# Loading the first two x tiles as two column halves, and moving half of their transposes behind the first products

## The chip, the cores and the metric

One core of a Trainium2 chip runs the whole kernel. The metric is the device time of one execution in microseconds (us); lower is better. The kernel before has a median of 104.45 us over three runs (104.1, 104.45 and 105.25).

A core has five engines that run side by side and meet through semaphores: TensorE (PE, with its weight loads listed apart as PEld), VectorE (DVE), ScalarE (ACT), GpSimd (POOL) and SyncE (SP). Transfers between the large memory and the core's own memory are issued here from two rings, SyncE's (SP) and ScalarE's (ACT), and all of them run on the same 16 DMA engines.

## The reference

A dense layer, the Mish activation, and a second dense layer. x is 2048 x 512, w1 is 512 x 1792, w2 is 1792 x 512, all bf16:

```python
h = einsum("bsd,df->bsf", x, w1) + b1
sp = log1p(exp(-abs(h))) + where(h > 0, h, 0)
act = h * tanh(sp)
return einsum("bsf,fd->bsd", act, w2)
```

## The kernel before

The 2048 tokens are worked in four blocks of 512. For each block the first dense layer makes 14 tiles `f` of 128 hidden columns; each is the sum of four products over `k`, the four 128-wide pieces of the 512 input columns (`mm1_step`, L189). ScalarE turns a finished tile into its activation (`mish`, L172). Then the second dense layer makes four token tiles, each a sum of 14 products of 512 columns (`mm2_step`, L212). Token tile 3 is the exception: its share of `f` = 1 is computed on VectorE (L230, L233) during the whole run and added at the end.

TensorE needs x with the input columns on the partitions, so x has to be transposed. For tokens 256 and up a transposing DMA does that. Tokens 0 to 255 (token tiles j = 0 and j = 1, the first to be needed) come in their natural layout by one plain load into `x_nat` (256 KB, L119) and are transposed by TensorE: `transpose_x` (L145) multiplies 64-row halves by a 64 x 64 identity, 16 instructions in all (L156), and VectorE and ScalarE copy the results from PSUM into `xT` (L164). The first products wait for these copies and for the first piece of w1.

The start of the kernel is written out by hand. Seven fills (L113) multiply constants into a PSUM bank that nobody reads; they keep TensorE busy until x arrives. w1's columns for `f` 0 to 7 (`OPEN` = 8) come as four loads of 256 KB, one per `k`: k 0 and k 2 on ScalarE's ring (L118), k 1 and k 3 on SyncE's (L120, L123). SyncE's ring carries, in this order: `x_nat`, k 1, the transposing load of tokens 256 to 511 (token tiles 2 and 3, `t_x23`, L122, which first waits for the third fill), k 3, b1, the rest of w1, and w2 in one load.

The products of block 0 are ordered by `first(fs, js, ks)`, which runs over k, then over f, for the token tiles in js: eight products of 128 columns (f 0 to 3, j 0, then j 1, k 0), then products of 256 columns for both j together (f 4 to 7 with k 0, then all eight f with k 1 and k 2), then 24 for token tiles 2 and 3 with k 0 to 2, and then eight of 512 columns with k 3, each of which completes a tile of `f`:

```python
first(range(4), (0,), (0,))
first(range(4), (1,), (0,))
first(range(4, OPEN), (0, 1), (0,))
first(range(OPEN), (0, 1), (1, 2))
first(range(OPEN), (2, 3), (0, 1, 2))
first(range(OPEN), None, (3,), True)
```

Tile `f` accumulates in PSUM bank `f % 8`; the transposes use banks 0 to 7 in pairs before that, and the first product into a bank waits for the copy that empties it.

## Time and profile before

| | us |
|---|---|
| median of three runs | 104.45 |
| the profiled execution | 104.08 |
| its span, first to last instruction | 102.7 |
| TensorE busy in it | 99.6 (97% of the span) |
| VectorE busy | 80.0 (78%) |
| ScalarE busy | 48.2 (47%) |
| DMA engines, moved in all | 24.76 MB at a mean of 241 GB/s |

The profile lists instructions with the line of the kernel that made them; a line can be that of a helper, so every load has line L93. Times are counted from the span's start. Matmuls are pipelined: the listed duration of one runs from its start to its modelled end and overlaps the next, so the rate of a stream of products is read from the distance of their starts. A few matmul records are missing from the trace. A share of the 16 DMA engines can come out above 100% in a short window, since a packet counts whole where it starts.

### The profile page before, as it was taken

The numbers are of one execution on the slowest core, as the hardware profiler recorded it, in microseconds if no ns is written. First come the engines' busy times: TensorE is split into PE (matmuls) and PEld (weight loads), VectorE is DVE, ScalarE is ACT, GpSimd is POOL, SyncE is SP. The second block draws the span as 40 slices with busy tenths as digits, with TensorE's granted clock in tenths as the row PEclk, the third lists the DMA queues.
The fourth block names the chain that finished last, engine by engine and source line by source line (L and its number), as shares of the span: only waits on it lengthen the run. The fifth ranks groups of instructions, "written<-read, shape, count | busy, mean of one in ns | idle before, by whom it ended". The sixth has DMA issues, their size and how long they took to land.

```text
span 102.7 us, 1352 instructions
## 1 busy us (share of the span) xinstructions
PE 99.6 (97%) x518; PEld 48.7 (47%) x527; DVE 80.0 (78%) x142; ACT 48.2 (47%) x75; POOL 0.4 (0%) x5
## 2 busy tenths in 40 slices
PE   6999999999999999999999999999999999999993
PEld 2587444444444444444444444444444444444472
DVE  1203000695979599999999999999999999999972
ACT  4301999220777781022588872222277776210210
POOL 1000000000000000000000000000000000000000
PEclk9999999999999999999999999999999999999999
DMA  2999999999799999789496838497857839111103
GB/s 62 371 281 359 366 262 360 255 330 228 303 273 228 378 429 373 201 325 297 184 320 172 338 73 364 105 347 224 293 153 306 284 124 341 67 57 51 51 0 102
DMA packets 15442, 24.76 MB, mean 241 GB/s; under 512 B 8396, under 2 KB 12748, under 8 KB 13388
## 3 DMA queue, kind: packets, MB, share of 16 engines
q1 hardware_dynamic: 15004, 24.12, 72.8%
q10 hardware_dynamic: 432, 0.56, 1.5%
q8 instruction: 4, 0.07, 0.2%
q14 instruction: 2, 0.02, 0.1%
HBM read 20.71 MB, written 2.10 MB: 222 GB/s over the span
## 4 chain that ended last, share of the span: by engine, by line
PE 97%; issue 1%; DVE 0%
PE ps L189 47%; PE ps L212 47%; PE ps L113 3%; PE ps L156 1%; DVE o_sb L271 0%
## 5 line engine op out<-in xcount | busy, mean ns | idle before, releaser
L233 DVE SCALAR_TENSOR_TENSOR acc<-w_bc,a_tok,acc 128x448 f32<-128x448 bf16 x126 | 75.4, 681 | 3.0 <-DMA w_bc<-in_w_dram 3.0
L189 PE MATMUL ps<-xT,w_sb 128*128 128x512 bf16 (+2 forms) x247 | 48.8, 355 | 0.4
L212 PE MATMUL ps<-w_sb,a_sb 128*128 128x512 bf16 (+3 forms) x248 | 48.7, 354 | 0.2
L172 ACT ACTIVATE a_sb<-ps,b_sb 128x512 bf16<-128x512 f32 x56 | 37.2, 698 | 12.8 <-PE ps L189 7.6
L189 PEld LDWEIGHTS ps<-xT,w_sb 128*128 128x128 bf16 x252 | 24.2, 98 | 24.2 <-DVE xT L164 0.3
L212 PEld LDWEIGHTS ps<-w_sb,a_sb 128*128 128x128 bf16 x252 | 23.1, 98 | 25.5 <-issue 0.3
L247 ACT ACTIVATE o_sb<-ps 128x512 bf16<-128x512 f32 x14 | 8.4, 598 | 32.7 <-PE ps L212 32.7
L230 DVE TENSOR_SCALAR acc<-w_bc,a_tok 128x448 f32<-128x448 bf16 x2 | 0.8, 450 | 10.4 <-DMA w_bc<-in_w_dram 10.4
L113 PE MATMUL ps<-const-bfloat16-1.0 128*128 128x512 bf16 (+1 forms) x7 | 2.7, 563 | 0.8 <-PEq L355 0.8
L289 DVE STREAM_TRANSPOSE b_T<-b_nat 32x32 bf16<-32x32 bf16 x4 | 0.8, 202 | 3.3 <-DMA b_nat<-in_b_dram 3.2
L164 DVE CAST xT<-ps 128x128 bf16<-128x128 f32 (+1 forms) x2 | 0.6, 352 | 2.4 <-PE ps L156 2.4
L271 ACT ACTIVATE o_sb<-ps 128x320 bf16<-128x320 f32 x1 | 0.4, 438 | 4.1 <-PE ps L212 4.1
L113 PEld LDWEIGHTS ps<-const-bfloat16-1.0 128*128 128x128 bf16 x7 | 0.9, 135 | 2.1 <-issue 2.1
L164 ACT ACTIVATE xT<-ps 128x256 bf16<-128x256 f32 (+1 forms) x3 | 0.9, 347 | 1.8 <-PE ps L156 1.7
L115 ACT ACT_TABLE_LOAD x1 | 1.3, 1283 | 0.7 <-PEq L355 0.7
L271 DVE CAST o_sb<-ps 128x128 bf16<-128x128 f32 (+1 forms) x2 | 0.5, 258 | 1.1 <-PE ps L212 1.0
L110 DVE MEMSET b_nat<- 32x64 uint32 x1 | 0.1, 112 | 0.8 <-PEq L355 0.8
L243 DVE TENSOR_TENSOR o_sb<-ps,acc 128x448 bf16<-128x448 f32 x1 | 0.6, 625 | 0.1
L241 DVE TENSOR_TENSOR acc<-acc 128x448 f32<-128x448 f32 x1 | 0.6, 624 | 0.0
L156 PEld LDWEIGHTS ps<-ident,x_nat 64*128 64x128 bf16 x16 | 0.5, 123 | 0.4 <-DMA x_nat<-in_x_dram 0.4
L156 PE MATMUL ps<-ident,x_nat 64*128 64x64 bf16 x16 | 0.6, 237 | 0.0
L139 DVE TENSOR_SCALAR ident<-diff 128x128 bf16<-128x128 int32 x1 | 0.2, 227 | 0.2 <-POOL diff L137 0.2
(7 smaller groups left out, 1.0 us busy)
## 6 DMA issues: line engine op xcount, KB each, us to landing
w_bc<-in_w_dram SPq DMA_DIRECT2D x16, 1024.0 KB, 4.9
out_dram<-o_sb SPq DMA_DIRECT2D x15, 128.0 KB, 2.3
w_sb<-in_w_dram SPq DMA_DIRECT2D x1, 1792.0 KB, 11.0
w_sb<-in_w_dram SPq DMA_DIRECT2D x1, 768.0 KB, 5.8
w_sb<-in_w_dram ACTq DMA_DIRECT2D x2, 256.0 KB, 3.7
w_sb<-in_w_dram SPq DMA_DIRECT2D x2, 256.0 KB, 3.6
x_nat<-in_x_dram SPq DMA_DIRECT2D x1, 256.0 KB, 2.6
out_dram<-o_sb SPq DMA_DIRECT2D x1, 80.0 KB, 1.6
```

The lines of the kernel that those rows point to most:

```text
L113: t_fill = [pe.mark(nc.tensor.matmul(ps[:, 7, 0:n], c_w, c_m[:, 0:n], start=True, stop=True)) for n in WARM]
L115: act.eng.preload_act_table(ACT.Mish)
L156: mm = nc.tensor.matmul(ps[:, b0 + h, lo:lo + H], x_nat[g, j, k * P:(k + 1) * P], ident[g, g], start=True, stop=True)
L164: t = eng.mark(nc.vector.tensor_copy(dst, src) if eng is dve else act.eng.activation(dst, src, ACT.Copy))
L172: t = act.mark(act.eng.activation(a_sb[:, f, starts[s]:starts[s + 1]], ps[:, bank, 0:n], ACT.Mish, bias=b1_sb[:, f:f + 1]))
L189: return nc.tensor.matmul(ps[:, bank, lo:hi], w1_sb[:, k, f * P:(f + 1) * P], xT[:, k, starts[s] + lo:starts[s] + hi], start=first, stop=( ...
L212: return nc.tensor.matmul(ps[:, bank, c:hi - lo], a_sb[:, f, i * P:(i + 1) * P], w2_sb[:, f, lo + c:hi], start=(f == 0), stop=(f == FT - 1))
L230: t = dve.mark(nc.vector.tensor_scalar(o, w, col, None, ALU.mult))
L233: t = dve.mark(nc.vector.scalar_tensor_tensor(o, w, col, o, ALU.mult, ALU.add))
L247: t = [act.mark(act.eng.activation(dst, src, ACT.Copy))]
L271: t = eng.mark(nc.vector.tensor_copy(dst, src) if eng is dve else act.eng.activation(dst, src, ACT.Copy))
L289: t = dve.mark(nc.vector.transpose(b1_T[j * SQ:(j + 1) * SQ, :], b1_nat[:, j * SQ:(j + 1) * SQ]))
```

## The change

The load of `x_nat` is cut into two loads, columns 0 to 255 (k 0 and 1) and columns 256 to 511 (k 2 and 3), each with its own semaphore. The load of w1's k 1 moves from SyncE's ring to ScalarE's. `transpose_x` does k 0 and 1 alone; one fill of 256 columns (`KEEP`) follows it, and one of the fills ahead of it is dropped and another made shorter. After the first eight products TensorE waits for the second half of `x_nat` and transposes its four 128 x 128 tiles (k 2 and 3, j 0 and 1) in whole tiles into bank 6; ScalarE copies them out in two instructions. Since bank 6 is taken by then, the products of `f` = 6 with k 0 and k 1 come after those of the other seven.

```diff
-WARM = (512,) * 5 + (256,) * 2
+WARM = (512,) * 5 + (128,)
+KEEP = (256,)
...
-        for k in (0, 2):
+        for k in (0, 1, 2):
             load_part(act, k, k + 1, 0, OPEN)
-        t_xn = load(sp, x_nat[:, :, :], x2[0:2 * P, :].rearrange("(p j) d -> p j d", p=P), "s_xn")
-        load_part(sp, 1, 2, 0, OPEN)
+        xv = x2[0:2 * P, :].rearrange("(p j) d -> p j d", p=P)
+        t_xn = [load(sp, x_nat[:, :, c:c + D // 2], xv[:, :, c:c + D // 2], "s_xn%d" % c) for c in (0, D // 2)]
         sp.wait(t_fill[2])
...
-            for b0, eng, js, ks in ((0, dve, (0,), (0,)), (2, act, (1,), (0,)), (4, dve, (0, 1), (1,)), (6, act, (0, 1), (2, 3))):
+            for b0, eng, js, ks in groups:
...
-        transpose_x()
+        transpose_x(t_xn[0], ((0, dve, (0,), (0,)), (2, act, (1,), (0,)), (4, dve, (0, 1), (1,))))
+        for n in KEEP:
+            fill(n)
         t_b1c = spread_b1()
         first(range(4), (0,), (0,))
         first(range(4), (1,), (0,))
-        first(range(4, OPEN), (0, 1), (0,))
-        first(range(OPEN), (0, 1), (1, 2))
+        pe.wait(t_xn[1])
+        for k in (2, 3):
+            for j in (0, 1):
+                lo = (k - 2) * 2 * P + j * P
+                mm = nc.tensor.matmul(ps[:, 6, lo:lo + P], x_nat[:, j, k * P:(k + 1) * P], ident[:, :], start=True, stop=True)
+        act.wait(pe.mark(mm))
+        for k in (2, 3):
+            t = act.mark(act.eng.activation(xT[:, k, 0:2 * P], ps[:, 6, (k - 2) * 2 * P:(k - 1) * 2 * P], ACT.Copy))
+            t_cp[0, k] = t_cp[1, k] = t
+        free[6] = [t]
+        first((4, 5, 7), (0, 1), (0,))
+        first((0, 1, 2, 3, 4, 5, 7), (0, 1), (1,))
+        first((6,), (0, 1), (0, 1))
+        first(range(OPEN), (0, 1), (2,))
```

TensorE's queue at the start of the program, before the change (a name is output <- input; `ps` is PSUM, and the last number of a shape is the columns):

```order
L113 MATMUL ps<-const-bfloat16-1.0 128x512 x5
L113 MATMUL ps<-const-bfloat16-1.0 128x256 x2
L156 MATMUL ps<-ident,x_nat 128x64 x16
L189 MATMUL ps<-xT,w_sb 128x128 x8
L189 MATMUL ps<-xT,w_sb 128x256 x44
L189 MATMUL ps<-xT,w_sb 128x512 x32
```

And with the change:

```order
L116 MATMUL ps<-const-bfloat16-1.0 128x512 x5
L116 MATMUL ps<-const-bfloat16-1.0 128x128
L161 MATMUL ps<-ident,x_nat 128x64 x8
L116 MATMUL ps<-const-bfloat16-1.0 128x256
L194 MATMUL ps<-xT,w_sb 128x128 x8
L308 MATMUL ps<-ident,x_nat 128x128 x4
L194 MATMUL ps<-xT,w_sb 128x256 x44
L194 MATMUL ps<-xT,w_sb 128x512 x32
```

Eight of the sixteen half transposes are gone from ahead of the products, four whole ones stand between the eighth and the ninth product, and the products themselves are the same in number and size; a fill of 256 columns stands just ahead of the first product.

SyncE's queue at the start, which issues only transfers, before the change:

```order
L93 DMA x_nat<-in_x_dram 128x1024
L93 DMA w_sb<-in_w_dram 128x1024
L93 DMA_TRANSPOSE xT<-in_x_dram 128x4x256
L93 DMA w_sb<-in_w_dram 128x1024
L93 DMA b_nat<-in_b_dram 14x128
L93 DMA w_sb<-in_w_dram 128x4x768
L93 DMA w_sb<-in_w_dram 128x14x512
```

And with the change:

```order
L94 DMA x_nat<-in_x_dram 128x2x256 x2
L94 DMA_TRANSPOSE xT<-in_x_dram 128x4x256
L94 DMA w_sb<-in_w_dram 128x1024
L94 DMA b_nat<-in_b_dram 14x128
L94 DMA w_sb<-in_w_dram 128x4x768
L94 DMA w_sb<-in_w_dram 128x14x512
```

The first load is now two, and its pieces are runs of 256 elements (512 bytes) where they were runs of 1024 elements (2048 bytes); the load of w1's k 1 that stood second is gone from this queue, and ScalarE issues three such loads, k 0, 1 and 2, where it issued two.

More of the change, by code (lines that the diff above doesn't have):

```diff
@@ L112, in bass_standalone__dense_activation_mish__prompt_kernel, with fill @@
         c_m = nc.const_aps.tensor(1.0, [P, 512], BF)
-        t_fill = [pe.mark(nc.tensor.matmul(ps[:, 7, 0:n], c_w, c_m[:, 0:n], start=True, stop=True)) for n in WARM]
+        def fill(n):
+            return nc.tensor.matmul(ps[:, 7, 0:n], c_w, c_m[:, 0:n], start=True, stop=True)
+        t_fill = [pe.mark(fill(n)) for n in WARM]
         act.eng.preload_act_table(ACT.Mish)
         act.wait(t_bz)
-        for k in (0, 2):
+        for k in (0, 1, 2):
             load_part(act, k, k + 1, 0, OPEN)
-        t_xn = load(sp, x_nat[:, :, :], x2[0:2 * P, :].rearrange("(p j) d -> p j d", p=P), "s_xn")
-        load_part(sp, 1, 2, 0, OPEN)
+        xv = x2[0:2 * P, :].rearrange("(p j) d -> p j d", p=P)
+        t_xn = [load(sp, x_nat[:, :, c:c + D // 2], xv[:, :, c:c + D // 2], "s_xn%d" % c) for c in (0, D // 2)]
         sp.wait(t_fill[2])
@@ L143, in bass_standalone__dense_activation_mish__prompt_kernel, with transpose_x @@
         t_mish = {}
-        def transpose_x():
-            pe.wait(t_xn, t_id)
+        def transpose_x(t, groups):
+            pe.wait(t, t_id)
             H = P // 2
-            for b0, eng, js, ks in ((0, dve, (0,), (0,)), (2, act, (1,), (0,)), (4, dve, (0, 1), (1,)), (6, act, (0, 1), (2, 3))):
+            for b0, eng, js, ks in groups:
                 m = len(js)
```

## The prediction

> **What bounds the kernel now.** I read the page first, then the chain of waits in order of time, then the start instruction by instruction. The page says how little there is to win:
>
> ```profile
> PE 99.6 (97%) x518; PEld 48.7 (47%) x527; DVE 80.0 (78%) x142; ACT 48.2 (47%) x75; POOL 0.4 (0%) x5
> ```
>
> The chain of waits (start, length, who) shows where TensorE (PE) is not yet on products:
>
> ```profile
> 0.77 2.71 PE ps L113 x7
> 3.49 0.54 PE ps L156 x16
> 4.03 0.13 issue
> 4.16 5.42 PE ps L189 x52
> 9.58 0.05 issue
> 9.64 6.85 PE ps L189 x31
> ```
>
> Fills, then the transposes, then from 4.16 us products without a break (the pieces of 0.05 are missing records). So the end moves one for one with two things: the start of the first product, and whatever TensorE does after it that is not a product. The change touches both.
>
> What releases the first product stands in three views: the timeline of the start, the DMA issues one by one (KB, us from issue to landing), and the groups by shape for the copies.
>
> ```profile
> 0.74 0.40 SPq L93 DMA_DIRECT2D x_nat<-in_x_dram  x1
> 0.95 0.86 ACTq L93 DMA_DIRECT2D w_sb<-in_w_dram  x2
> 1.20 0.41 SPq L93 DMA_DIRECT2D w_sb<-in_w_dram  x1
> 1.36 0.46 ACTq L93 DMA_DIRECT2D w_sb<-in_w_dram  x1
> 2.24 1.30 SPq L93 DMA_TRANSPOSE xT<-in_x_dram  x1
> 5.18 0.50 SPq L93 DMA_DIRECT2D w_sb<-in_w_dram  x1
> ...
> 3.70 0.62 DVE L164 CAST xT<-ps 128x128 bf16<-128x128 f32 x2 [2.38 <-PE ps L156]
> 3.75 0.98 ACT L164 ACTIVATE xT<-ps 128x128 bf16<-128x128 f32 x3 [1.73 <-PE ps L156]
> ...
> x_nat<-in_x_dram SPq DMA_DIRECT2D x1, 256.0 KB, 2.6
> w_sb<-in_w_dram ACTq DMA_DIRECT2D x1, 256.0 KB, 3.1
> w_sb<-in_w_dram SPq DMA_DIRECT2D x1, 256.0 KB, 3.5
> w_sb<-in_w_dram ACTq DMA_DIRECT2D x1, 256.0 KB, 4.3
> xT<-in_x_dram SPq DMA_TRANSPOSE x1, 4.3
> w_sb<-in_w_dram SPq DMA_DIRECT2D x1, 1792.0 KB, 11.0
> ...
> L164 DVE CAST xT<-ps 128x128 bf16<-128x128 f32 x1 | 0.3, 291 | 2.4 <-PE ps L156 2.4
> ```
>
> Issue plus landing time: x_nat at 3.34, k 0 (0.95) at 4.05, k 1 (1.20) at 4.70, k 2 (1.36) at 5.66, the transposed tiles 2 and 3 (2.24) at 6.54, w2 (5.18) at 16.18. VectorE's first copy ends at 3.70 + 0.29 = 3.99. So **two things** release the first product at 4.16, about 0.1 us earlier: the copy at 3.99 and k 0 at 4.05. Bringing x forward alone would do nothing; k 0 has to move too.
>
> **The transfers.** They run one after another at full rate. In windows of the DMA view (packets, MB, share of 16 engines) only one ring is at work:
>
> ```profile
> q1 hardware_dynamic: 67, 0.14, 103.7%
> q10 hardware_dynamic: 79, 0.16, 101.3%
> q1 hardware_dynamic: 672, 0.17, 127.8%
> ```
>
> The first is 3.68 to 4.02 us (SyncE's ring, w1 k 1), the second 4.36 to 4.80 (ScalarE's, k 2), the third 5.14 to 5.74 (SyncE's, the transposing load). A packet of 2048 bytes takes 1.037 x 16 x 0.34 / 67 = 84 ns of one engine, one of 256 bytes 1.278 x 16 x 0.60 / 672 = 18 ns. The change makes x's packets 512 bytes, which no row shows. On the straight line between these two it is 28 ns; the bounds are 18 and 84. I take 28, since 512 lies near the 256 end.
>
> - x_nat took 128 x 84 / 16 = 0.67 us of all engines. One half is 256 packets of 28 ns: 0.45 us. So the first half is through 0.22 us earlier, and k 0 behind it also.
> - Both halves take 0.90 us, so everything behind them is **0.22 us later**: k 2 at 5.88, tiles 2 and 3 at 6.76, w2 at 16.40. k 1 loses its place to the second half and follows it: 4.70 + 0.22 = 4.92. That second half lands 0.45 behind k 0: 3.83 + 0.45 = 4.28.
>
> First half at 3.12, VectorE's first copy at 3.77, k 0 at 3.83: the first product starts at 4.16 - 0.22 = **3.94**. The fills are out of the way: five of 512 columns and one of 128 end near 3.0 (next rows). The added fill of 256 columns runs while the copies do.
>
> **The clock.** The page's PEclk row reads full speed throughout, but the distances do not:
>
> ```profile
> 2.43 0.15 PEld L113 LDWEIGHTS ps<-const-bfloat16-1.0 128*128 128x128 bf16 x1 [0.28 <-issue]
> 2.86 0.15 PEld L113 LDWEIGHTS ps<-const-bfloat16-1.0 128*128 128x128 bf16 x1 [0.28 <-issue]
> 3.42 0.24 PE L156 MATMUL ps<-ident,x_nat 64*128 64x64 bf16 x2
> 3.79 0.24 PE L156 MATMUL ps<-ident,x_nat 64*128 64x64 bf16 x2
> 4.16 0.23 PE L189 MATMUL ps<-xT,w_sb 128*128 128x128 bf16 x1
> 4.39 0.50 PE L189 MATMUL ps<-xT,w_sb 128*128 128x128 bf16 x5
> 4.83 0.49 PE L189 MATMUL ps<-xT,w_sb 128*128 128x256 bf16 x3
> 5.71 0.49 PE L189 MATMUL ps<-xT,w_sb 128*128 128x256 bf16 x3
> 15.89 0.59 PE L189 MATMUL ps<-xT,w_sb 128*128 128x512 bf16 x2
> 16.33 0.38 PE L212 MATMUL ps<-w_sb,a_sb 128*128 128x512 bf16 x1
> ```
>
> Fills of 512 columns stand 0.43 us apart; products of 512 later 0.22 (15.89 to 16.33 holds two), of 256 0.11 (4.83 to 5.71 holds eight), of 128 from 4.16 on 0.057 (four by 4.39). The transposes still ran at half speed: eight pairs of 64 columns from 3.42 to 3.79, 0.053 a pair. So full speed came between 3.8 and 4.2, just as the products began: the products start free of the slow stretch by a hair. A start at 3.94 lies in it.
>
> I take the grant at 4.18. From 3.94 to 4.18 products of 128 take 0.11 us: 2.2 of the eight. The other 5.8 take 0.32, so the eight end at **4.50**, where before they ended at 4.16 + 8 x 0.057 = 4.62. Of the 0.22 us of head start 0.12 is left. Were the grant at 3.9, all of it would be.
>
> The Trainium skill (TensorE: Matmul & The Clock Gate, Part 1: The HAM clock gate) has the same rule: half clock until TensorE has been busy for a window of about 3.4 us; 0.77 + 3.4 = 4.2 agrees with the spacings. It also calls the window free-running, so that the moment varies from run to run; one trace cannot show that.
>
> **The transposes in the stream.** Ahead of the products, transposes cost nothing, since the first product waits for VectorE and k 0. Behind the eighth product they are TensorE time: four of 128 columns at the products' rate, 4 x 0.057 = **0.23 us**. The wait ahead of them is free: the half is there at 4.28, the eight end at 4.50. ScalarE's two copies end well ahead of the products with k 2: ScalarE starts 0.33 after TensorE's first transpose in the rows above (3.42 to 3.75) and needs 0.98 for three copies, so near 5.8; the first product that needs them or bank 6 comes later, as follows.
>
> **The sum on TensorE.** After: eight products by 4.50, transposes to 4.73, then the same 44 of 256 columns. Before these began at 4.62. Net **+0.11 us**. Then the later transfers have to be in time:
> - k 1 is wanted at 4.73 + 3 x 0.11 = 5.06 and lands at 4.92: 0.14 ahead, where a landing released a product after some 0.1.
> - bank 6 and k 2 are wanted after 12 products, at 6.05; k 2 lands at 5.88 and frees a product at 5.98.
> - tiles 2 and 3: wanted at 6.93, there at 6.76.
> - w2: the first L212 moves from 16.33 to 16.44; w2 lands at 16.40 and frees it at 16.50. Before, it had 0.15 to spare, now it is 0.06 late.
>
> No cover is more than 0.1 us thick, so I add 0.05 for the most likely miss: **+0.16 us**. VectorE's chain for tile 3 starts up to 0.22 later; at its end there is more room than that:
>
> ```profile
> L271 DVE CAST o_sb<-ps 128x128 bf16<-128x128 f32 x1 | 0.3, 292 | 1.0 <-PE ps L212 1.0
> ```
>
> VectorE sat idle for 1.0 us before the last copies.
>
> The sum against the profiled execution: 104.08 + 0.16 = 104.24. Its 104.08 is 0.37 under the median of the three runs; against the median the forecast is 104.45 + 0.16 = **104.6**.
>
> **The rivals.**
>
> *Slower: k 2 falls behind the transposing load.* Before, the rings alternated: x (SP), k 0 (ACT), k 1 (SP), k 2 (ACT), tiles 2 and 3 (SP). The windows above show whole transfers in turn, which fits two rules, order of issue or turn by turn between the rings; before, both give the same sequence. With the change SP holds both halves and then tiles 2 and 3, ACT holds k 0, 1, 2. By order of issue k 2 (issued near 1.8) stays ahead; turn by turn it is half, k 0, half, k 1, *tiles 2 and 3*, k 2. The transposing load moves 262144 / 256 = 1024 packets, 1024 / 672 x 0.60 = 0.91 us. Then k 2 lands at 5.88 + 0.91 = 6.79, its product starts at 6.89 instead of 6.05: a hole of 0.84, with the 0.11 a total of +0.95: **105.4**. If the load gives way after a part of its packets, the hole shrinks; under a fifth of them none is left. Against it: nothing in the trace of before. For it also nothing: it decides at k 1's end, and before that case never arose. The Trainium skill (DMA: Bandwidth & Descriptors, Queues, rings and completion order) says that an engine alternates between rings packet by packet, a packet being some 9 to 17 pieces and at most 64; no run so far shows it. By that rule a part of the load, up to all of it, goes first.
>
> *Slower still: full speed comes one stretch later.* From the first fill to the grant were 3.4 us. The fills ahead of x shrink from 3072 columns to 2688 plus 256 behind the transposes, and there is a pause for x near 3.0 and one for k 0. If that leaves TensorE too idle for the grant at 4.2, another 3.4 us run at half speed: 1.7 us of products lost, **106.2**. Against it: the pauses sum to about 0.5 of 3.4 us.
>
> *512-byte packets are dear.* At 42 ns a half takes 0.67 like the whole before: the first product stays at 4.16, the second half lands at 4.72 and is late by 0.2 with the eight done at 4.62, k 1 (5.37) by another 0.15, and 0.23 for the transposes: **105.0**. At 84 ns it would be over a microsecond. This is the case in which the change doesn't bring x forward at all.
>
> *A clear gain.* The grant comes by 3.9, or packets cost 18 ns (k 0 0.38 earlier, start 3.78): the eight end at 4.24 to 4.39, the sum is between 0 and -0.15: **104.3**. More isn't there, since k 0 must land in any case.
>
> **How the numbers follow.** Forecast (104.6, own range 104.2 to 105.0) 0.50; k 2 behind the load 0.22; dear packets 0.08; the grant a stretch later 0.07; clear gain 0.13. The range 104.0 to 105.4 takes in the first, the gain, the dear packets and half of the second. A difference of about 1%, 1.04 us, is what runs that spread from 104.1 to 105.25 can tell from none. No case gives a gain of that size; scatter alone: 0.03. Slower by over 1% are the late grant and some two fifths of the k 2 case: 0.16. The rest, 0.81, is within 1%.
>
> **What would show it.** In the profile after: the first product near 3.94, its first two or three at 0.11 distance; four transposes right behind the eighth product without a gap; the first 512-column product of block 0 about 0.1 later than before. k 2 landing at 5.9 says order of issue, at 6.2 to 6.8 with idle time of TensorE ahead of a product near 6 says turn by turn. A half landing later than 3.3 says dear packets. Products at 0.22 for 256 columns after 4.3 us say late grant. I am wrong in the main if the stretch up to the first L212 changes by more than 0.3 us with none of these.

## The result and the profile after

The changed kernel takes **108.34 us** in the median of six runs (107.66 to 108.92). The kernel before took 104.5 in six runs beside it (104.1 to 105.25). The ratio is **1.035**, with a 95% interval of 1.029 to 1.041: slower by 3.8 us, where 0.16 was forecast, and well outside the range given. Runs more than 1.5% above the fastest of the same kernel count as slow, and the ranges and ratios from here on leave them out. The profiled execution took 108.65 us, with a span of 107.3 against 102.7; the two traces are thus 4.6 us apart, somewhat more than the medians.

The page of the kernel after, busy time of the engines:

```profile
PE 102.6 (96%) x514; PEld 50.4 (47%) x523; DVE 80.0 (75%) x142; ACT 48.1 (45%) x75; POOL 0.4 (0%) x5
```

VectorE and ScalarE do as much as before. TensorE is busy 3.0 us more, although it has the same products: the same work has become slower, and the rest is idle time. The chain of waits of the kernel after, in order of time (start, length, who):

```profile
0.73 0.66 SPq L94
1.46 5.00 DMA x_nat<-in_x_dram
6.51 0.61 PE ps L308 x4
7.12 7.02 PE ps L194 x44
14.19 6.85 PE ps L194 x31
21.04 3.88 PE ps L217 x18
```

Before, the chain began with fills on TensorE. Now it begins with a transfer: the second half of x, which lands at 6.46 us. The chain comes to the first L217 at 21.04; before, it came to that place at 9.64 + 6.85 = 16.49. All of the difference between the traces, 4.55 us, lies ahead of it, and the stretch of 6.85 before it has kept its length. Where in these 21 us the loss is, the timeline of the kernel after shows (start, duration, what):

```profile
0.73 0.66 SPq L94 DMA_DIRECT2D x_nat<-in_x_dram  x1
1.46 0.59 SPq L94 DMA_DIRECT2D x_nat<-in_x_dram  x1
0.95 0.39 ACTq L94 DMA_DIRECT2D w_sb<-in_w_dram  x1
...
4.01 0.39 PE L161 MATMUL ps<-ident,x_nat 64*128 64x64 bf16 x8 [0.83 <-DMA x_nat<-in_x_dram]
...
4.63 0.39 PE L194 MATMUL ps<-xT,w_sb 128*128 128x128 bf16 x2
5.14 0.53 PE L194 MATMUL ps<-xT,w_sb 128*128 128x128 bf16 x3
6.51 0.29 PE L308 MATMUL ps<-ident,x_nat 128*128 128x128 bf16 x1 [0.84 <-DMA x_nat<-in_x_dram]
...
10.75 0.63 PE L194 MATMUL ps<-xT,w_sb 128*128 128x256 bf16 x2
11.57 0.49 PE L194 MATMUL ps<-xT,w_sb 128*128 128x256 bf16 x3
```

The row at 10.75, two products of 256 columns, lasts 0.63 us. One of them is listed with 0.42 (start to modelled end), so the second starts 0.21 after the first, where before it was 0.11. The starts stand about 0.21 apart up to 11.4 us and 0.11 apart from then on. Eight products of 128 columns take from 4.63 to 5.46 with 0.107 each, where before they had 0.057. So TensorE runs at half speed for seven more microseconds than before. The page of this execution has no row of the granted clock, and the windows below read 1.00 throughout; only the distances show it. In brackets stand two idle times that were not there before: 0.83 us ahead of the first transposes, 0.84 (by the modelled end) behind the eighth product, both released by x.

Counted back from 11.4 in stretches of 3.4 us (length, then busy time and instructions of PE, PEld, DVE, ACT and POOL, clock, mean, GB/s):

```profile
1.20:4.60 3.40, 2.56 (x15) 0.88 (x13) 0.43 (x3) 1.09 (x2) 0.00 (x0) 1.00 0.72 221
4.60:8.00 3.40, 2.56 (x19) 1.96 (x19) 0.31 (x1) 0.67 (x3) 0.00 (x0) 1.00 1.13 294
8.00:11.40 3.40, 3.40 (x18) 2.42 (x17) 0.98 (x5) 0.00 (x0) 0.00 (x0) 1.00 1.08 363
```

Each of the first two holds one of the pauses; the third is the first that is busy throughout, and at its end full speed comes. Where such stretches begin I only infer from that end.

The pieces add up, each as the kernel after against the one before:

| | before | after | difference, us |
|---|---|---|---|
| start of the first product | 4.16 | 4.63 | 0.47 |
| eight products of 128 columns | 0.46 | 0.83 | 0.37 |
| idle until the second half of x lands and frees TensorE | 0 | 5.46 to 6.51 | 1.05 |
| four transposes of 128 columns, at half speed | 0 | 0.40 | 0.40 |
| 44 products of 256 columns, 22 of them at half speed | 4.80 | 7.06 | 2.26 |
| sum | | | 4.55 |

By cause: the slow clock costs 0.37 + 0.18 (the transposes beyond 4 x 0.056) + 2.26 = 2.8 us, the transfers and the transposes' own length 0.47 + 1.05 + 0.22 = 1.7.

The single DMA issues of the kernel after (KB, us from issue to landing), in the order first half, second half, k 0, k 1, k 2, tiles 2 and 3:

```profile
x_nat<-in_x_dram SPq DMA_DIRECT2D x1, 128.0 KB, 3.2
x_nat<-in_x_dram SPq DMA_DIRECT2D x1, 128.0 KB, 5.0
w_sb<-in_w_dram ACTq DMA_DIRECT2D x1, 256.0 KB, 2.6
w_sb<-in_w_dram ACTq DMA_DIRECT2D x1, 256.0 KB, 3.7
w_sb<-in_w_dram ACTq DMA_DIRECT2D x1, 256.0 KB, 4.6
xT<-in_x_dram SPq DMA_TRANSPOSE x1, 5.2
```

With the issues' starts (0.73 and 1.46 for the halves, 0.95, 1.34 and 1.85 for the three pieces of w1), the first half lands at 3.96, k 0 at 3.58, k 1 at 5.03, the second half at 6.46, k 2 at 6.45. Half of x takes longer to come than all of x did, and w1's k 0, issued 0.22 us behind it, is there 0.4 ahead of it. The reason shows in windows of the DMA view (packets, MB, share of 16 engines; q1 is SyncE's ring, q10 ScalarE's). The first line is from 1.78 to 2.6 us, the next two from 2.96 to 3.3, the last three from 4.8 to 5.3:

```profile
q10 hardware_dynamic: 62, 0.13, 65.1%
...
q1 hardware_dynamic: 179, 0.09, 89.1%
q10 hardware_dynamic: 18, 0.02, 15.4%
...
DMA packets 139, 0.17 MB, mean 339 GB/s; under 512 B 33, under 2 KB 68, under 8 KB 139
q10 hardware_dynamic: 76, 0.15, 80.5%
q1 hardware_dynamic: 63, 0.02, 18.1%
```

Until 2.6 us nothing of x has moved. And the transfers do not run one after another: in the third window 76 packets of k 1 and k 2 and 63 of SyncE's ring go side by side, the latter mostly pieces of 512 bytes of the second half and of 256 bytes of the transposing load behind it (33 in all are under 512 bytes, a few of them of 4). The counts are alike, but w1's packets have 2048 bytes, so that SyncE's ring gets 0.02 of 0.17 MB.

### The profile page after: what moved, and what is told of

Same layout as the page of the kernel before. It is cut to its first block, busy times and chain, and to the rows that moved or that the text cites. A ratio compares the mean times of both kernels' runs of the same rounds, so it can differ in the third digit from the quotient of the medians.

```text
span 107.3 us, 1345 instructions
## 1 busy us (share of the span) xinstructions
PE 102.6 (96%) x514; PEld 50.4 (47%) x523; DVE 80.0 (75%) x142; ACT 48.1 (45%) x75; POOL 0.4 (0%) x5
## 4 chain that ended last, share of the span: by engine, by line
PE 92%; DMA 5%; issue 1%; SPq 1%; DVE 0%
PE ps L194 47%; PE ps L217 45%; DMA x_nat<-in_x_dram 5%; SPq L94 1%; PE ps L308 1%; DVE o_sb L276 0%
## 5 line engine op out<-in xcount | busy, mean ns | idle before, releaser
L194 PE MATMUL ps<-xT,w_sb 128*128 128x512 bf16 (+2 forms) x247 | 51.7, 371 | 0.3
L217 PE MATMUL ps<-w_sb,a_sb 128*128 128x512 bf16 (+3 forms) x248 | 48.7, 354 | 0.2
L194 PEld LDWEIGHTS ps<-xT,w_sb 128*128 128x128 bf16 x252 | 25.8, 104 | 25.1 <-DVE xT L169 0.2
L217 PEld LDWEIGHTS ps<-w_sb,a_sb 128*128 128x128 bf16 x252 | 23.2, 98 | 25.4
L116 PE MATMUL ps<-const-bfloat16-1.0 128*128 128x512 bf16 (+2 forms) x7 | 2.8, 545 | 0.8 <-PEq L374 0.8
L311 ACT ACTIVATE xT<-ps 128x256 bf16<-128x256 f32 x2 | 0.7, 381 | 2.5 <-PE ps L308 2.5
L308 PE MATMUL ps<-ident,x_nat 128*128 128x128 bf16 x4 | 0.6, 308 | 0.8 <-DMA x_nat<-in_x_dram 0.8
```

Of the source, the lines that this page charges most:

```text
L116: return nc.tensor.matmul(ps[:, 7, 0:n], c_w, c_m[:, 0:n], start=True, stop=True)
L194: return nc.tensor.matmul(ps[:, bank, lo:hi], w1_sb[:, k, f * P:(f + 1) * P], xT[:, k, starts[s] + lo:starts[s] + hi], start=first, stop=( ...
L217: return nc.tensor.matmul(ps[:, bank, c:hi - lo], a_sb[:, f, i * P:(i + 1) * P], w2_sb[:, f, lo + c:hi], start=(f == 0), stop=(f == FT - 1))
L308: mm = nc.tensor.matmul(ps[:, 6, lo:lo + P], x_nat[:, j, k * P:(k + 1) * P], ident[:, :], start=True, stop=True)
```

## The experiments

The first theory after the result: the column halves themselves are slow to land, and the pause that they leave costs TensorE its full clock. Its rivals: w1's k 1 on the other ring is what delays them; the transposes in the stream and the fewer fills are to blame; or the 512-byte packets are dear. Every kernel below computes the whole result; a fill only adds products that nobody reads. Ratios are against the kernel before on the same chip, with their 95% interval.

**1. The pauses filled, as far as they go: the clock's share.** The kernel after with more fills ahead of x, and with fills of 2048 columns in all while TensorE waits for the second half:

```diff
-WARM = (512,) * 5 + (128,)
+WARM = (512,) * 7 + (128,)
+COVER = (512,) * 4
...
         first(range(4), (1,), (0,))
+        for n in COVER:
+            fill(n)
         pe.wait(t_xn[1])
```

> The changed kernel with fills put into TensorE's two pauses (two more ahead of the first half of x, four behind the eighth product); transfers untouched. Theory 'transfers first' (the halves of x come late, 3.96 and 6.46 us in the profile of the changed kernel, and the pauses that this makes also cost the full clock until 11.4 us): full speed comes near 4.2 us, the second half still lands near 6.4, the first product of 512 columns near 11.5 instead of 14.0, time about 106.4 us. Rival 'clock alone' (the transfers cost nothing by themselves): about 104.6. Rival 'the clock has nothing to do with the pauses': 108.3 as the changed kernel.

106.45 us (106.44 to 106.47), ratio 1.019 (1.017 to 1.022). The chain of waits of this kernel:

```profile
1.46 5.29 DMA x_nat<-in_x_dram
6.79 0.40 PE ps L311 x4
7.18 11.71 PE ps L195 x76
```

The second half comes no earlier (1.46 + 5.29 = 6.75), yet all 76 products behind the transposes now take 11.7 us, where after they took 21.04 - 7.12 = 13.9. The rows by window from 7.00 to 10.40 us, columns as above, first of the kernel after, then of this one:

```profile
7.00:10.40 3.40, 3.40 (x19) 2.42 (x17) 0.98 (x5) 0.66 (x2) 0.00 (x0) 1.00 1.05 352
```

```profile
7.00:10.40 3.40, 3.40 (x35) 3.05 (x33) 0.98 (x5) 0.66 (x2) 0.00 (x0) 1.00 1.05 348
```

19 instructions against 35 in the same 3.4 us, both with TensorE "busy" throughout and the clock column at 1.00. So the slow clock is real and it followed from idle time: with most of the idle time filled, 1.9 of the 3.8 us are gone. Not all of it is filled. The four fills ran at full speed and were over early, so that 0.58 us (by the modelled end) were left ahead of the four transposes; full speed, which had come by 4.2, outlasted that pause. The other 1.9 are the transfers and the four transposes, and no clock brings them back. Its runs also spread least of all kernels here.

**2. All but the transfers.** The kernel after with x in one load and k 1 back on SyncE's ring; the transposes behind the eighth product, the order of the products and the fills stay as changed:

```diff
-        for k in (0, 1, 2):
+        for k in (0, 2):
             load_part(act, k, k + 1, 0, OPEN)
-        t_xn = [load(sp, x_nat[:, :, c:c + D // 2], xv[:, :, c:c + D // 2], "s_xn%d" % c) for c in (0, D // 2)]
+        t_xn = [load(sp, x_nat[:, :, :], xv, "s_xn")] * 2
+        load_part(sp, 1, 2, 0, OPEN)
```

> The changed kernel with both edits to the loads undone: x in one load, w1's k 1 on SyncE's ring; the moved transposes and the changed fills stay. 'Transfers first': x lands at 3.4, w1's k 0 at 4.0, no pause over 0.5 us, full speed near 4.2, time 104.5 to 105.0 (0.2 us for the transposes in the stream). Rival 'fewer fills ahead of x lose the clock by themselves': products at half speed beyond 7 us, 106 us or more.

105.22 us (104.34 to 105.86), ratio 1.006 (1.002 to 1.009), a little above the 105.0 expected. The chain: eight products, four transposes, and on without a break.

```profile
4.20 1.01 PE ps L195 x8
5.21 0.43 PE ps L309 x4
5.64 11.80 PE ps L195 x76
```

In this execution (105.01 us) full speed came near 5.7, so the twelve instructions ran at half speed. The lowest run, 104.34, is 0.21 above the lowest of before beside it (104.13), which is what four transposes cost at full speed. The moved transposes and the fills are worth some 0.6 us, not 3.8.

**3. The split load alone.** The kernel before with x in two column halves, all transposes waiting for both:

```diff
-        t_xn = load(sp, x_nat[:, :, :], x2[0:2 * P, :].rearrange("(p j) d -> p j d", p=P), "s_xn")
+        xv = x2[0:2 * P, :].rearrange("(p j) d -> p j d", p=P)
+        t_xn = [load(sp, x_nat[:, :, c:c + D // 2], xv[:, :, c:c + D // 2], "s_xn%d" % c) for c in (0, D // 2)]
...
```

> The kernel before with x in two column halves on SyncE's ring and nothing else; the transposes wait for both. 'Transfers first', with the split load itself as the cause: the second half lands 1 to 3 us later than x did (4.4 to 6.4 against 3.4), time 105.5 to 109. Rival 'the third load on ScalarE's ring crowds x out, the split is harmless': landing by 3.7, time 104.5 to 104.9.

107.71 us (107.45 to 108.54), ratio 1.033 (1.028 to 1.037): nearly the whole loss, from this edit alone. The chain:

```profile
0.74 3.36 DMA x_nat<-in_x_dram
4.10 1.36 issue
5.46 0.61 PE ps L157 x16
```

The halves land at 4.10 and 5.37 (the second waits behind k 0 and for its own late start), and the transposes begin at 5.46 instead of 3.42.

**4. The ring alone.** The kernel before with k 1 on ScalarE's ring, x in one load:

```diff
-        for k in (0, 2):
+        for k in (0, 1, 2):
             load_part(act, k, k + 1, 0, OPEN)
...
-        load_part(sp, 1, 2, 0, OPEN)
```

> The kernel before with w1's k 1 on ScalarE's ring and nothing else. If the split load is the cause: x at 3.4 and k 0 at 4.0 as before, k 1 near 4.8, time 104.4 to 104.8. Rival 'the third load on ScalarE's ring is the cause': x or k 1 lands over a microsecond later, time above 105.5. If the rings take turns transfer by transfer, the transposing load of tiles 2 and 3 goes ahead of k 1 by 0.9 us: k 1 near 5.6, time near 105.1.

104.57 us (104.34 to 105.07), ratio 1.001 (0.999 to 1.004). x lands at 3.37, k 0 at 4.06, k 1 at 4.93, k 2 at 6.01. By itself this part is harmless; as long as x goes in one load, k 1 and k 2 come in time from either ring.

**5. What makes a half slow: bytes per packet, or runs per partition?** A column half differs from the whole in two ways. Its pieces are 512 bytes, and each partition takes two pieces (one per token tile) where the whole had one. Three loads of x pull these apart, each in the kernel before. Two token halves: one piece of 1024 bytes per partition. Four quarters: one piece of 512. And one load whose destination rows are padded by 32 columns, so that every partition takes two pieces of 1024 bytes:

```diff
+        t_xn = [load(sp, x_nat[:, j, :], xv[:, j, :], "s_xn%d" % j) for j in (0, 1)]
...
```

> The kernel before with x in two loads of one token tile each: 128 runs of 1024 bytes a load, one run per partition; the transposes wait for both. Theory 'the form of the split load' (two runs per partition, or runs of 512 bytes, make a load slow to set out): the first half sets out like x before (lands near 3.1 us) and the second one comes behind w1's k 0, near 4.0; time 104.9 to 106. Rival 'any second load on the ring, whatever its form, makes both late': landings near 4.1 and 5.4 as with column halves, time 107.5 to 108.

```diff
+        t_xn = [load(sp, x_nat[:, j, c:c + D // 2], xv[:, j, c:c + D // 2], "s_xn%d_%d" % (c, j)) for c in (0, D // 2) for j in (0, 1)]
...
```

> The kernel before with x in four loads of 64 KB, each one token tile by half the columns: 128 runs of 512 bytes, one run per partition. Rival 'runs of 512 bytes are what is slow': the first quarter lands no earlier than 3.6 us, with few of its packets moved by 2.5. Theory 'two runs per partition are what is slow to issue and to set out': the first quarter sets out near 1.8 us and lands by 3.0, and each issue takes 0.4, not 0.66. The last quarter is issued near 2.1 and lands behind k 0 and k 2 in any case (4.5 to 5.5), time 106 to 108.

```diff
-        x_nat = sb("x_nat", [P, 2, D], BF)
+        x_nat = sb("x_nat", [P, 2, D + 32], BF)
...
+        t_xn = load(sp, x_nat[:, :, 0:D], xv, "s_xn")
```

> The kernel before with x in one load, as before 256 KB, but into rows with a gap between the two token tiles, so that it is 256 runs of 1024 bytes, two per partition. Theory 'two runs per partition are slow': the issue takes 0.66 us, x lands behind k 0, at 4.1 or later, time 105.3 to 107.5. Rival 'runs of 512 bytes are slow': x lands at 3.4 as before, time 104.5.

The timeline's row of the issue and the landings of the two token halves:

```profile
0.74 0.40 SPq L93 DMA_DIRECT2D x_nat<-in_x_dram  x1
```

```profile
x_nat<-in_x_dram SPq DMA_DIRECT2D x1, 128.0 KB, 2.3
x_nat<-in_x_dram SPq DMA_DIRECT2D x1, 128.0 KB, 3.0
```

The first of the four quarters is issued in 0.40 us as well, and lands at 2.75.

The padded load, its issue and its landing:

```profile
0.73 0.66 SPq L93 DMA_DIRECT2D x_nat<-in_x_dram  x1
```

```profile
x_nat<-in_x_dram SPq DMA_DIRECT2D x1, 256.0 KB, 3.5
```

For these loads the runs decide, and not the bytes of a piece. With one run per partition the issue takes 0.40 us, and the first load of x lands at 3.0 (128 KB in pieces of 1024 bytes) or at 2.75 (64 KB in pieces of 512). With two, the issue takes 0.66 us, and x lands at 4.25, in pieces of 1024 bytes, behind k 0 (3.48), which was issued later. Packets of 512 bytes are not dear: the quarters set out as early as the whole. Two things stay open. A load with two runs per partition also has 256 pieces instead of 128, and nothing here tells these two apart. And it is no rule for every load: in the kernel before, the rest of w1, with four runs per partition, is issued in 0.41 us, and w2, with 14, in 0.50.

The times: the padded load took 104.96 to 107.23 in ten runs, two of them below 105 and eight above 106.4; its ratio of 1.010 (1.004 to 1.017) rests on the four lowest, and its trace is of a run of 106.91. The quarters took 107.62 us, 1.027 (1.022 to 1.033), since four issues from one queue bring the last quarter in only at 5.39, and the transposes here wait for all of it. The token halves took 104.76 in one run and 106.5 to 107.3 in three, too far apart for a ratio. What a late landing costs depends on the clock: in the trace of the token halves (104.76) x is complete at 4.16, in that of the padded load (106.91) at 4.25, hardly later; but from 6 to 8 us TensorE does 21 instructions in the first and 11 in the second, which is at half speed until 9.2. The quarters show the clock at its plainest. Windows of 3.4 us from 3.60 on, columns as above:

```profile
3.60:7.00 3.40, 1.18 (x27) 1.06 (x28) 0.62 (x2) 0.83 (x3) 0.00 (x0) 1.00 1.12 292
7.00:10.40 3.40, 3.40 (x18) 2.42 (x17) 0.98 (x5) 0.00 (x0) 0.00 (x0) 0.50 0.97 317
10.40:13.80 3.40, 3.40 (x30) 2.73 (x28) 0.00 (x0) 0.16 (x1) 0.00 (x0) 1.00 1.09 369
```

TensorE was busy for 1.18 us of the first window. In the next one, busy throughout, the granted clock is 0.50 and 18 instructions get through; then it is 1.00 again. The loss comes one window after the idle time and lasts one window.

**6. How the two late causes share out.** Two kernels. In the first (from the kernel after) k 1 goes back behind the halves on SyncE's ring. In the second (from experiment 3) ScalarE's loads are held back until the fifth fill, so that x is alone; k 0 comes late in it, so that its time doesn't say what the halves cost.

```diff
-        for k in (0, 1, 2):
+        for k in (0, 2):
             load_part(act, k, k + 1, 0, OPEN)
...
+        load_part(sp, 1, 2, 0, OPEN)
```

> The changed kernel with w1's k 1 back on SyncE's ring, behind both halves. If the rings take turns packet by packet, the second half has to share with k 2 alone instead of k 1 and k 2, as in the kernel with the halves alone: it lands near 5.4 instead of 6.46, the pause behind the eighth product is gone or under 0.3 us, time 106.3 to 107.5. If transfers run in order of issue, nothing changes for the second half: 6.4, time near 108.3.

```diff
-        act.wait(t_bz)
+        act.wait(t_bz, t_fill[4])
...
```

> The kernel before with x in two column halves on SyncE's ring, and ScalarE's loads (w1's k 0 and k 2) held back until the fifth fill is done, near 3.1 us, so that nothing else is on the DMA engines while the halves set out; ScalarE's ring is empty until then. 'Two runs per partition are slow to issue and to set out': the first half still takes 0.66 us to issue, moves nothing before 2.7 us, and lands at 3.3 to 3.6; the second one at 3.8 to 4.1. Rival 'w1's k 0 crowds the halves out': the first half moves from 1.8 us and lands by 2.9. k 0 comes late in any case (near 5), so the time, 106 to 108, tells nothing.

The first: 106.89 us (106.65 to 107.2), ratio 1.021 (1.015 to 1.028), with the second half landing at 5.79, where 5.4 was expected. In the kernel after it was 6.46, in experiment 3, which has the same loads in the same rings, 5.37. So 0.7 us of it is k 1's doing, and 0.4 have no cause that I can show: in these loads the two kernels are the same. Each is a single execution; with the loads of the kernel after, the second half of experiment 1 landed at 6.74, 0.3 later than there. The pause behind the eighth product shrinks from 0.84 to 0.18 (by the modelled end) and full speed comes near 8.2 instead of 11.4. So the ring, harmless with x in one load, counts when the second half has to share with it.

The second: landing of the first half, then the DMA view from 1.0 to 2.0 and from 2.0 to 2.6.

```profile
x_nat<-in_x_dram SPq DMA_DIRECT2D x1, 128.0 KB, 2.6
```

```profile
DMA packets 0, 0.00 MB, mean 0 GB/s; under 512 B 0, under 2 KB 0, under 8 KB 0
...
q1 hardware_dynamic: 151, 0.08, 42.5%
```

With nothing beside it the first half lands at 3.37 and sets out near 2.2, against 1.8 for the whole load before. So the late start by itself is 0.4 us; my "nothing before 2.7" was wrong. The rest, from 3.37 to 3.96, is k 0 going ahead of it. How k 0 holds it back is open: the engines were not full, k 0 took 65% of them from 1.78 to 2.6 in the kernel after. The packet price forecast holds: 0.425 x 16 x 0.60 / 151 = 27 ns for 512 bytes, where the forecast took 28.

The one run of this kernel took 113.04 us, where 106 to 108 was expected, because k 0 came far later than thought: issued at 3.16 on ScalarE's ring, it landed at 10.50 and not near 5. It went beside the transposing load on SyncE's. From 5 to 6 us the 23 packets of ScalarE's ring took 99.8% of the 16 engines' time, 0.69 us each where a packet of 2048 bytes took 0.084 in the kernel before, and both rings together moved 79 GB/s. The two hinder each other here by far more than sharing; the same comes up again in experiment 8.

**7. A repair.** If runs per partition are the cause, quarters with one run each, spread over both rings, should give the change what it was meant to have. From the kernel after; the second variant also has the fills of before:

```diff
-        for k in (0, 1, 2):
-            load_part(act, k, k + 1, 0, OPEN)
-        t_xn = [load(sp, x_nat[:, :, c:c + D // 2], xv[:, :, c:c + D // 2], "s_xn%d" % c) for c in (0, D // 2)]
+        t_xn = [[quarter(sp, 0, 0), quarter(act, 1, 0)], []]
+        load_part(sp, 0, 1, 0, OPEN)
+        t_xn[1] = [quarter(act, 0, 1), quarter(sp, 1, 1)]
+        for k in (1, 2):
+            load_part(act, k, k + 1, 0, OPEN)
...
```

(`quarter(q, j, c)` loads column half c of token tile j from ring q.)

> The changed kernel with its idea kept and the form of the loads mended: x in four loads of 64 KB with one run of 512 bytes per partition, SyncE's ring carrying (j 0, first columns), w1's k 0, (j 1, second columns), ScalarE's (j 1, first columns), (j 0, second columns), k 1, k 2. Theory: the two first quarters land by 3.2, k 0 by 4.0, the first product starts at 3.8 to 4.1, no pause behind the eighth product, and the sum of the prediction (+0.1 to +0.2) is what is left, with up to 0.4 more where the clock comes late, as with the moved transposes alone: 104.6 to 105.2. Rival 'more loads at the start are slow whatever their form': first product after 4.4, time above 105.6.

```diff
-WARM = (512,) * 5 + (128,)
-KEEP = (256,)
+WARM = (512,) * 5 + (256,) * 2
+KEEP = (128,)
```

> As the mended kernel, with the fills ahead of x as they were before the change (five of 512 and two of 256 columns) and 128 columns behind the transposes instead of 256. If the cut fills cost clock by themselves, this is 0.2 to 0.5 us faster than the mended kernel (104.3 to 104.6); if not, the two are the same within 0.2.

The repair: ratio 1.011 (1.006 to 1.017), with two of six runs outside of it at 107.4 and 107.5; with the fills of before 1.012 (1.007 to 1.016), with one of six outside at 120.95. The quarters wanted first land at 2.73 and 2.95, k 0 at 3.94, the first product starts at 4.08, and there is no pause behind the eighth. Two thirds of the loss is repaired, and the number of fills is no part of it. But it is still 1.2 us slower than before, more than the 0.8 that was expected at most. Three more kernels look for the rest.

**8. A short pause ahead of the first product?** The repair leaves TensorE idle for a moment ahead of the first product. One kernel fills it (the repair with twice the fill, `KEEP = (256,) * 2`); two test such pauses in the kernel before, by fewer fills ahead of x and by more:

> The mended kernel (four quarter loads, one run per partition) with twice the fill between its transposes and its first product, so that TensorE's pause of about 0.3 us there is closed. Theory 'the share of a window in which TensorE is idle decides when the full clock comes, so a pause of a few tenths ahead of the products moves it by a window in some executions': median 0.5 us or more under the mended kernel's (105.6 in its undisturbed executions), near 104.6 to 105.0. Rival 'the pause doesn't matter, the mended kernel is slow for another reason': 105.4 to 105.9.

```diff
-WARM = (512,) * 5 + (256,) * 2
+WARM = (512,) * 5 + (128,)
```

> The kernel before with the fills ahead of x cut as the change cuts them (128 columns in place of two times 256) and nothing else: a pause of 0.3 to 0.4 us ahead of the transposes. 'The share of idle time decides': slower than before by 0.2 to 0.8 us, by executions in which full speed comes later, none faster than 104.1. Rival 'such a short pause doesn't matter': same median as before, 104.5.

```diff
-WARM = (512,) * 5 + (256,) * 2
+WARM = (512,) * 5 + (256,) * 2 + (128,)
```

> The kernel before with 128 columns more of fill ahead of x, which closes the 0.1 us left there, and nothing else. 'The share of idle time decides': the same or up to 0.2 us faster in the median (104.3 to 104.5), the fastest executions unchanged at 104.1. If the added fill delays the transposes, up to 0.1 us slower.

The repair with its pause filled 105.54 us (105.35 to 105.75), 1.009 (1.006 to 1.011). The kernel before with fewer fills 104.58, 1.000 (0.997 to 1.003); with more 104.79, 1.002 (0.999 to 1.005). A pause of 0.3 us ahead of the transposes, which fewer fills leave, costs nothing, so the pause is not it. What the trace of the filled repair shows instead are late transfers. Windows of the DMA view from 5.4 to 6.8, first of the kernel before, then of this one:

```profile
q1 hardware_dynamic: 712, 0.42, 113.2%
```

```profile
q1 hardware_dynamic: 462, 0.12, 89.3%
q10 hardware_dynamic: 67, 0.11, 26.0%
```

k 2 (0.11 MB on ScalarE's ring) now goes beside the transposing load (0.12 MB on SyncE's), and together they move 0.23 MB where 0.42 went before. From 5 to 7 us the rate is 187 GB/s against 291. k 2 lands at 7.08 (before 5.66), tiles 2 and 3 at 8.04 (before 6.54). The holes of TensorE ahead of the products that need them, at 7.12 and 8.09, are only 0.1 us each, but whatever comes behind on SyncE's ring is late too, and the last of it binds: w2. Its row in the DMA view (issued at 5.17), and the first product of the second layer in the timeline:

```profile
w_sb<-in_w_dram SPq DMA_DIRECT2D x1, 1792.0 KB, 12.5
17.83 0.38 PE L224 MATMUL ps<-w_sb,a_sb 128*128 128x512 bf16 x1
```

w2 lands near 17.7, where before it landed at 16.18. The product that needs it starts at 17.83. The one ahead of it starts at 17.41 and lasts 0.22, so TensorE waited 0.2 us for w2. In the kernel before that product starts at 16.33, 1.50 earlier, and the two profiled executions are 105.54 - 104.08 = 1.46 apart. Full speed came near 6.2 in this one; had it come sooner, TensorE would have waited longer for w2, which fits the narrow range of its runs (eight of nine; the ninth took 107.58). So the prediction's first rival is real on the transfers, but its price is paid at w2.

**9. k 2 on SyncE's ring ahead of the transposing load.** From the filled repair:

```diff
-        for k in (1, 2):
-            load_part(act, k, k + 1, 0, OPEN)
+        load_part(act, 1, 2, 0, OPEN)
+        load_part(sp, 2, 3, 0, OPEN)
         sp.wait(t_fill[2])
```

> The mended kernel with the closed pause, and w1's k 2 on SyncE's ring ahead of the transposing load instead of on ScalarE's ring beside it. Theory 'the mended kernel's microsecond is k 2 and the transposing load of tiles 2 and 3 slowing each other down, since the rings take turns' (there k 2 landed at 7.1 and the tiles at 8.0 us, with holes of TensorE before both): k 2 lands by 6.1, the tiles by 7.0, time 104.3 to 104.9, with the spread of the kernel before. Rival 'four loads in place of one make everything behind them late': k 2 after 6.6, time 105.2 to 105.7.

The windows from 5 to 7 us, first of the filled repair, then of this kernel:

```profile
5.00:7.00 2.00, 2.00 (x17) 1.58 (x14) 0.00 (x0) 0.66 (x2) 0.00 (x0) 1.00 1.06 187
```

```profile
5.00:7.00 2.00, 1.93 (x19) 1.51 (x17) 0.00 (x0) 0.62 (x2) 0.00 (x0) 1.00 1.19 278
```

On the transfers the theory holds: k 2 lands at 5.95 instead of 7.08, tiles 2 and 3 at 6.98 instead of 8.04, at 278 GB/s, and w2 at 16.5 instead of 17.7. On the time it does not: four of its runs lie between 104.44 and 105.91, ratio 1.011 (1.006 to 1.017), and three more took 106.04 to 107.71. The profiled execution is the best of them, 104.44, so the trace does not show what the slower ones lack. A hole of 0.24 us ahead of k 1's products (k 1 lands at 5.28) is in it, and the four transposes are in the stream; why the other runs are a microsecond and more longer **stays open**.

A part of it may be the moment of full speed. Four profiled executions have the same products, starting between 4.16 and 4.26, and no transfer holds these up after that:

| kernel | full speed comes near, by the distances | time of that execution, us |
|---|---|---|
| before | 4.2 | 104.08 |
| fewer fills (experiment 8) | 5.0 | 104.50 |
| k 1 on ScalarE's ring (experiment 4) | 5.3 | 104.59 |
| more fills (experiment 8) | 6.4 | 105.17 |

Each microsecond of delay costs half a microsecond, which is what products at half speed lose. In this kernel's best execution full speed came by 4.1. That it came later in the others is argued, not shown, and by the table it would explain a microsecond, not the three of the slowest. No version made here beats the kernel before.

## Why the prediction was wrong

**"The transfers": here it failed.** The packet price was right (27 ns against 28). But it was the only thing the step asked about a smaller load. It let the halves set out at the same time as the whole, with k 0 between them, each transfer "at full rate": 3.12 and 4.28. They landed at 3.96 and 6.46. The difference has three parts, each shown by a run. The load with two runs per partition takes 0.66 us to issue instead of 0.40 and sets out 0.4 us late (experiments 5 and 6; alone it lands at 3.37 instead of 3.12). In that time k 0 on the other ring goes ahead, worth 0.6 us (3.37 alone, 3.96 with k 0). And the second half, issued later still, shares its time with k 1 and k 2 from the other ring (6.46, 5.79 with k 1 moved back, 5.37 without the change of rings; of the last 0.4 I have no clean account). The premise that "they run one after another" came from windows in which one ring had work. It was read as a rule, and both rings side by side appear in the very first window of the changed kernel in which both had work. (In the trace of before they do so where one load ends and the next begins: 61 packets of SyncE's ring and 28 of ScalarE's from 2.6 to 3.0.) The row that should have warned stands in SyncE's queue with the change: `128x2x256` where `128x1024` stood.

The Trainium skill (DMA: Bandwidth & Descriptors, Queues, rings and completion order) says that a DMA engine goes round the rings that have work, packet by packet. The prediction used that for k 2 alone. The window from 4.8 to 5.3 (76 and 63 pieces of the two rings) agrees with turns; how many pieces one turn has it does not show. Applied to the second half, with as many pieces a turn for both rings, the rule would have said that pieces of 512 bytes lose their share to pieces of 2048.

**"The clock": right as a mechanism, missed as a case.** The step set the grant at 4.18, so that the products start free of the slow stretch "by a hair", and it gave the rival of one stretch later a chance of 0.07, because "the pauses sum to about 0.5 of 3.4 us". The pauses were 0.83 us ahead of the transposes and 0.84 (1.05 by distance) behind the eighth product, both from the late halves, and full speed came near 11.4, two stretches of 3.4 late (4.6 + 2 x 3.4 = 11.4, with the stretches as counted above). The price given, 1.7 us, was for one; the measured one is 1.9 by experiment 1 and 2.8 in the traces. The two estimates were made independent of each other, and they are not: a late transfer is also what makes TensorE idle enough to lose the clock. That coupling is what turned 1.7 us of late transfers and transposes into 4.55 between the two traces.

**"The transposes in the stream": the price was right, the wait was not.** 0.23 us was forecast; the lowest runs of experiment 2 differ by 0.21, and in experiment 1, at full speed, the four run from 6.79 to 7.02. At half speed they cost 0.40. "The wait ahead of them is free" followed from the second half at 4.28; with its landing at 6.46 the wait was 1.05 us.

**"The sum": its later links were not put to the test** in this kernel, since everything stood behind the pause. In the repairs they were. In the filled repair k 2 lands at 7.08 beside the transposing load, where the first rival said 6.79, so on the transfers this rival is real. That the kernel is 1.0 us above the one before, where the rival said 0.95, is luck: the hole was to be 0.84 us ahead of k 2's products, and it is 0.1; the time is set by the last link of the sum, w2, which lands 1.5 us later than before.

**"What would show it": one sign pointed the wrong way.** "A half landing later than 3.3 says dear packets." It landed at 3.96 with cheap packets. A landing time alone cannot tell a slow transfer from one that started late; the start of the packets in the DMA view can. The sign for the late grant (products at 0.22 for 256 columns after 4.3 us) was right.

## What to carry to other kernels

A load that is cut smaller is not only fewer bytes: look at its form too. Here a second run per partition made the issue longer and the start later, and a load from another ring that was behind went ahead. Transfers that wait in two rings went side by side here, packet by packet, so a load that the critical path waits for should have long runs and nothing wanted later in the other ring beside it; and a transposing load beside a plain one made both late, with all that follows them. And where a kernel lives off a full TensorE clock from its first product, a landing that is late by a microsecond costs a second time in products at half speed; price the two together, and read the speed from the distance of the products, not from the clock row.

## What the runs showed of the hardware

- x as the first load of SyncE's ring, two runs per partition: 0.66 us of issue instead of 0.40, for halves of 512-byte and for a whole of 1024-byte runs alike. The halves' first packets came 1.4 us after the start of the issue with nothing beside them and 2.1 with k 0 beside them; those of the whole with one run came after 1.0. Other loads with more runs were issued faster (w2, with 14, in 0.50).
- A transposing load and another ring's plain load, side by side, moved 187 GB/s from 5 to 7 us in the filled repair and 79 GB/s from 5 to 6 us in the second kernel of experiment 6; with the two one after the other it was 278 and 291 from 5 to 7 us.
- In the quarters of experiment 5 the full clock was lost after a stretch of 3.4 us in which TensorE was busy for 1.18 us, and it came back 3.4 us later. In the kernel after it did not come while stretches of 3.4 us held pauses of 0.8 us (2.56 busy); in the first kernel of experiment 6 it came after one with a pause of 0.18 (3.22 busy), and in experiment 1 a pause of 0.58 us did not end it. The Trainium skill (TensorE: Matmul & The Clock Gate, Part 1: The HAM clock gate) gives 3.4 us as the window; the row with 0.50 for just that long agrees. It calls the window free-running; full speed coming anywhere from 3.6 to 6.4 us in kernels that begin alike fits, and with it, by the table of experiment 9, the spread of 104.1 to 105.5 of the kernel before.
- A pause of 0.3 us in front of the first transposes did not cost anything (1.000, 0.997 to 1.003).
- The clock column read 1.00 for a stretch of the kernel after in which TensorE did 19 instructions, where a kernel at full speed did 35.
